# Taking the attention output out of PSUM with one ScalarE copy, and splitting it from SBUF

## The chip, the cores and the metric

The kernel runs on 1 core of one Trainium2 chip. The metric is the device time of one execution in microseconds (us); lower is better. The kernel before takes 699.35 us, the median of 3 runs (699.1 to 699.65).

## The reference

The computation is a sigmoid attention followed by a gated MLP with a spatial (token-mixing) gate, all in float32.

```python
# q, k, v: batch 8, 12 heads, 448 tokens, head dimension 64
scores = scale * np.matmul(q, k.transpose(0, 1, 3, 2)) - np.log(S)
attn = 1.0 / (1.0 + np.exp(-scores))
x = np.matmul(attn, v)            # then heads are joined: (8, 448, 768)

h = np.maximum(x @ w_in, 0.0)     # w_in: 768 x 1024
u, v = (h[..., :512], h[..., 512:])
v_n = (v - mean(v)) / np.sqrt(var(v) + 1e-06)
v_s = np.einsum('ts,bsd->btd', w_spatial, v_n) + b_spatial[None, :, None]
out = (u * v_s) @ w_out           # w_out: 512 x 768
```

## The kernel before

**Stages.** The eight batches are taken two at a time; the loop variable `m` counts the four pairs of batches. For each `m` the attention of both batches is computed into the SBUF tensor `x_s`, and then the MLP runs from `x_s`: `gate_values` (the half `v`, in PSUM tile `pv`), `spatial` (`pg`), `gated` (the half `u`, in `pu`) and `output` (`po`). The first attention pair of the next `m` is laid between the last outputs of this one.

**Precision.** Wide matmuls use operands in fp32r, and each operand is kept as a high part (the value rounded to fp32r) and a low part (the value minus the high part). `split(hi, lo, src, copy)` makes both: line 98 is the copy to the high part, on the engine that the caller names, and line 99 is a VectorE subtraction for the low part. The three products high*high, low*high and high*low are then added in PSUM.

**One attention step.** A unit is two heads of one batch; a batch has six units, and a step takes two units. So there are three steps for a batch, six for each `m`, and 24 in all. A step has seven score tiles, called here s (64 keys left over from both units, `t == NFULL`), e0, e1, e2 (the first unit) and o0, o1, o2 (the second). For each, `attention_scores` issues matmuls into a PSUM tile `psc` (line 251 for s, line 269, six matmuls a tile, for the others) and one ScalarE sigmoid (line 277) from there to an SBUF tile `at`. Then `attention_values` multiplies all seven `at` tiles with the values into one PSUM tile `pav` (line 295, 32 matmuls) in the order e0, e1, e2, o0, o1, o2, s; `pav` holds the first unit in one bank and the second in another. At its end `pav` is split into `x_s`, one unit after the other (lines 303 to 305): ScalarE makes the high part from PSUM, and VectorE the low part from PSUM and the high part.

**Buffers.** All PSUM tiles (`psc`, `pav`, `pv`, `pg`, `pu`, `po`) come from one pool of four buffers of two banks each, taken in turn. A step allocates eight of them, so `pav` stands in the buffer that e2 of the next step takes; o0, o1, o2 and the next `pav` take the buffers of that step's own s, e0, e1 and e2. The `at` tiles come from a pool `big` of `BIG = 7` SBUF buffers, taken in turn too; the tiles `vn` of `gate_values` come from the same pool.

**Order.** `in_program_order` keeps each engine's instructions in the order in which the program issues them. In one step that is: scores of s, e0, e1, e2, loads, scores of o0, o1, o2, in the first `m` a share of the weight preparation (`weigh`, on VectorE), the splits of q and k for the two units of the next step (`attention_splits`; the high part is made on ScalarE for batches 0 and 1 and on VectorE after that), and then `attention_values` with its split into `x_s`.

Of the kernel before, what the change touches and what calls it, by code (L numbers as in the profile page):

```python
# [8 lines left out]
F32 = mybir.dt.float32  # L9
# [5 lines left out]
P = 128  # L15
# [20 lines left out]
def attn_gmlp_kernel(  # L36
# [25 lines left out]
    nc = tc.nc  # L62
    B, NHP, _, _ = qk.shape
    S = out.shape[3]
# [15 lines left out]
    work = ctx.enter_context(tc.tile_pool(name="work", bufs=2))  # L80
# [7 lines left out]
    x_s = const.tile([P, 2, NCC, 2 * S], F32R, name="x_s")  # L88
# [8 lines left out]
    def split(hi, lo, src, copy):  # L97
        copy(hi, src)  # L98
        nc.vector.tensor_sub(lo, src, hi.bitcast(F32))  # L99

    def banks(name):
        return ps_2.tile([P, 2, 512], F32, tag="ps2", name=name)
# [3 lines left out]
    BIG = 7  # L106
# [173 lines left out]
    def attention_values(b, hp, ats):  # L280
        vt = values[b, hp]
        pav = banks(f"pav_{b}_{hp}")
        evens, odds = range(NFULL), range(NFULL + 1, TILES)
        for t in (*evens, *odds, NFULL):
            at = ats(t)
            for odd in range(2):
                if t == NFULL:
                    rows = slice(odd * HALF, (odd + 1) * HALF)
                elif (t > NFULL) == odd:
                    rows = slice(0, P)  # L290
                else:
                    continue
                for j in range(2):
                    heads = slice(j * D, (j + 1) * D)
                    nc.tensor.matmul(  # L295
                        pav[heads, odd, :S],
                        vt[rows, t, heads],
                        at[rows, j],
                        start=t == odd * (NFULL + 1),
                        stop=t == NFULL,  # L300
                    )
        cols = slice((b % 2) * S, (b % 2 + 1) * S)
        for odd in range(2):
            x, ps = x_s[:, :, hp + odd, cols], pav[:, odd, :S]
            split(x[:, 0], x[:, 1], ps, nc.scalar.copy)

    def product(ps, pairs, more=(), start=True, stop=True):

# [173 lines left out]
    def attention(m):  # L482
# [15 lines left out]
        for n in range(first, end, 2):  # L498
            if n:
                scores(n, short + evens)  # L500
            else:
                scores(n, evens)

            def loads():
                ahead(value_loads, n + 2, end)
                ahead(attention_loads, n + 4, end)
                ahead(attention_loads, n + 5, end)

            if n and n == first:
                yield  # L510
                attention_splits(*units[n + 1])
            if n:
                loads()
            scores(n, odds)
            if not n:
                scores(n, short)
            if n:
                weigh(WEIGH + (n + 2 == end))
            else:
                loads()  # L520
            ahead(attention_splits, n + 2, end)
            ahead(attention_splits, n + 3, end)
            if not n:
                weigh(1)
            attention_values(*units[n], lambda t: ats.pop((n, t)))
# [88 lines left out]
```

## Time and profile before

| | |
|---|---|
| median of 3 runs | 699.35 us |
| the profiled execution: its time / its span | 699.03 us / 697.2 us |
| TensorE matmul (PE) busy | 681.9 us, 98% of the span |
| TensorE weight load (PEld) busy | 505.9 us, 73% |
| VectorE (DVE) busy | 281.6 us, 40% |
| ScalarE (ACT) busy | 249.1 us, 36% |
| GpSimd (POOL) busy | 18.5 us, 3% |
| granted TensorE clock | 1.000 |

The span runs from the first to the last instruction, and the time of the execution has 1.83 us beside it. Matmuls are pipelined, so that the busy time of PE counts a matmul from its start to its modelled end, and several matmuls lie over one another. Idle time stands beside an instruction with the one that ended it. In the rows, "ACT x_s L98" is the copy to the high part of `x_s`, and "DVE x_s L99" the subtraction for its low part.

### The profile page before, as it was taken

The page shows a single profiled execution, that of the slowest core. Times are in us where ns is not written, and L with a number is a line of the kernel's source. Part 1 is how long each engine was busy: PE and PEld are TensorE (multiplying, and loading weights), DVE is VectorE, ACT ScalarE, POOL GpSimd, SP SyncE. Part 2 cuts the span into 40 slices and gives each one's busy share as a digit, 9 for nine tenths or more (in the row PEclk, how much of TensorE's full clock was granted, in tenths as well). Part 3 has the DMA queues.
Part 4 walks back from the last instruction along what each step waited for, and adds up shares of the span by engine and source line. Part 5 has one row for each costly group of instructions (what it writes and reads, how often), then busy time and mean ns, then how long its engine had stood idle before and what let it go on. Part 6 is the DMA issues. An engine that isn't in the chain of part 4 may idle for free.

```text
span 697.2 us, 9039 instructions
## 1 busy us (share of the span) xinstructions
PE 681.9 (98%) x3826; PEld 505.9 (73%) x3826; DVE 281.6 (40%) x445; ACT 249.1 (36%) x305; POOL 18.5 (3%) x36
## 2 busy tenths in 40 slices
PE   9999999999999999999999999999999999999997
PEld 3545789998645488999854458899985545889996
DVE  2767688833334037222242414621233431563020
ACT  5878322322466610011355741011136664101111
POOL 0000010000000001000000001100000000110000
PEclk9999999999999999999999999999999999999999
DMA  8754113160533000005062200000515410000102
GB/s 291 238 174 151 46 46 97 55 210 28 185 107 106 1 1 0 1 27 184 27 212 88 99 1 0 1 1 26 185 54 185 135 50 1 1 1 0 54 27 79
DMA packets 20552, 55.37 MB, mean 79 GB/s; under 512 B 1952, under 2 KB 8352, under 8 KB 20512
## 3 DMA queue, kind: packets, MB, share of 16 engines
q1 hardware_dynamic: 20224, 54.57, 23.0%
q8 instruction: 30, 0.49, 0.3%
q10 hardware_dynamic: 288, 0.23, 0.1%
q14 instruction: 10, 0.08, 0.0%
HBM read 43.78 MB, written 11.01 MB: 79 GB/s over the span
## 4 chain that ended last, share of the span: by engine, by line
PE 91%; DVE 4%; ACT 3%; issue 1%; DMA 0%
PE pav L295 20%; PE pu L311 17%; PE po L311 17%; PE pv L311 17%; PE psc L269 11%; PE pg L311 10%; DVE x_s L99 4%; ACT x_s L98 3%; PE psc L251 1%; DMA raw<-qk_dram 0%; DVE gs L99 0%; DVE g L428 0%; DVE osb L461 0%; ACT osb L459 0%; DVE gs L98 0%
## 5 line engine op out<-in xcount | busy, mean ns | idle before, releaser
L277 ACT ACTIVATE at<-psc,bias_s 128x896 f32<-128x896 f32 x168 | 153.9, 1026 | 22.1 <-PE psc L251 18.6
L295 PE MATMUL pav<-at,v 128*64 128x448 f32 (+1 forms) x768 | 135.4, 548 | 0.4
L311 PE MATMUL po<-gs,w_out_s 128*128 128x448 f32 x576 | 120.4, 368 | 1.0 <-DVE osb L461 0.9
L311 PE MATMUL pu<-x_s,w_in_s 128*128 128x448 f32 x576 | 118.0, 365 | 0.0
L311 PEld LDWEIGHTS po<-gs,w_out_s 128*128 128x128 f32 x576 | 107.7, 188 | 12.6 <-DVE osb L461 1.2
L311 PE MATMUL pv<-w_in_s,x_s 128*128 128x512 f32 x504 | 115.5, 390 | 0.0
L311 PEld LDWEIGHTS pu<-x_s,w_in_s 128*128 128x128 f32 x576 | 108.2, 188 | 8.6
L311 PEld LDWEIGHTS pv<-w_in_s,x_s 128*128 128x128 f32 x504 | 94.3, 188 | 22.3 <-issue 2.8
L269 PE MATMUL psc<-qks 64*128 64x448 f32 x828 | 99.1, 378 | 9.1 <-DVE x_s L99 9.1
L269 PEld LDWEIGHTS psc<-qks 64*128 64x128 f32 x828 | 75.4, 184 | 40.2 <-PE psc L269 16.1
L295 PEld LDWEIGHTS pav<-at,v 128*64 128x64 f32 (+1 forms) x768 | 44.2, 135 | 82.2 <-issue 62.0
L99 DVE TENSOR_TENSOR x_s<-pav,x_s 128x448 fp32r<-128x448 f32 x48 | 30.0, 625 | 142.4 <-ACT x_s L98 142.4
L311 PE MATMUL pg<-w_sp_s,vn 128*128 128x448 f32 x352 | 72.8, 365 | 0.0
L311 PEld LDWEIGHTS pg<-w_sp_s,vn 128*128 128x128 f32 x352 | 66.0, 187 | 5.8
L465 ACT COPY osb<-po 128x896 f32<-128x896 f32 x23 | 20.9, 907 | 114.4 <-PE po L311 97.8
L98 ACT CAST x_s<-pav 128x448 fp32r<-128x448 f32 x48 | 25.6, 532 | 86.2 <-PE pav L295 69.6
L99 DVE TENSOR_TENSOR qks<-raw,qks 128x832 fp32r<-128x832 f32 x46 | 46.7, 1025 | 19.3 <-ACT qks L98 18.1
L98 DVE CAST qks<-raw 128x832 fp32r<-128x832 f32 x36 | 21.2, 588 | 72.3 <-DMA raw<-qk_dram 37.1
L428 DVE SCALAR_TENSOR_TENSOR g<-pu,g 128x896 f32<-128x896 f32 x16 | 17.5, 1091 | 79.6 <-PE pu L311 79.6
L98 ACT CAST gs<-g 128x896 fp32r<-128x896 f32 x12 | 11.3, 943 | 99.0 <-DVE g L428 99.0
L346 ACT ACTIVATE rv<-pv 128x1024 f32<-128x1024 f32 (+1 forms) x16 | 14.6, 915 | 73.4 <-PE pv L311 73.4
L350 DVE BATCH_NORM_STATS2 stats<-rv 128x6 f32<-128x512 f32 x28 | 19.0, 679 | 38.4 <-ACT rv L346 38.4
(42 smaller groups left out, 243.3 us busy)
## 6 DMA issues: line engine op xcount, KB each, us to landing
raw<-qk_dram SPq DMA_DIRECT2D x48, 448.0 KB, 5.2
v<-v_dram SPq DMA_DIRECT2D x24, 448.0 KB, 3.3
out_dram<-osb SPq DMA_DIRECT2D x23, 448.0 KB, 2.6
wraw<-w_in_dram SPq DMA_DIRECT2D x12, 512.0 KB, 4.3
wraw<-w_out_dram SPq DMA_DIRECT2D x6, 512.0 KB, 3.6
wraw<-w_sp_dram SPq DMA_DIRECT2D x4, 256.0 KB, 4.8
b_bc<-b_sp_dram SPq DMA_DIRECT2D x1, 256.0 KB, 5.1
out_dram<-osb ACTq DMA_DIRECT2D x2, 112.0 KB, 1.7
```

The costliest lines, as they stand in the source:

```text
L98: copy(hi, src)
L99: nc.vector.tensor_sub(lo, src, hi.bitcast(F32))
L251: nc.tensor.matmul(psc[odd * HALF : (odd + 1) * HALF, j, :S], raw[rows, PART:], raw[rows, FULL:PART], start=True, stop=True,)
L269: nc.tensor.matmul(psc[:, j, :S], st[rows, k : k + P], mv[rows, FULL:PART], start=i == 0, stop=i == len(ops) - 1,)
L277: nc.scalar.activation(at, psc[:, :, :S], AF.Sigmoid, bias=bias_s, scale=QK)
L295: nc.tensor.matmul(pav[heads, odd, :S], vt[rows, t, heads], at[rows, j], start=t == odd * (NFULL + 1), stop=t == NFULL,)
L311: nc.tensor.matmul(ps, st, mv, start=start and i == 0, stop=stop and i == len(ops) - 1)
L346: nc.scalar.activation(rv[:, :n], pv[:, :n], AF.Relu)
L350: nc.vector.bn_stats(stats, rv[:, i])
L428: nc.vector.scalar_tensor_tensor(g, pu[:, :, :S], 0.0, g, op0=ALU.max, op1=ALU.mult)
L465: nc.scalar.copy(osb, po[:, :, :S])
```

## The change

In 20 of the 24 steps, one ScalarE copy takes both units' values (128 partitions by 896) from `pav` to a float32 tile `xf` in SBUF, which comes from the pool `big`; VectorE then makes the high part with a copy and the low part with a subtraction, both from `xf` and both over the two units at once. In the last step of each `m` (`hp + 2 == NHP` and an odd batch, 4 steps) there is no `xf`: the split reads PSUM as before, the high part on ScalarE and the low part on VectorE, but over both units in one instruction each.

```diff
         cols = slice((b % 2) * S, (b % 2 + 1) * S)
-        for odd in range(2):
-            x, ps = x_s[:, :, hp + odd, cols], pav[:, odd, :S]
-            split(x[:, 0], x[:, 1], ps, nc.scalar.copy)
+        x = x_s[:, :, hp : hp + 2, cols]
+        if hp + 2 == NHP and b % 2:
+            split(x[:, 0], x[:, 1], pav[:, :, :S], nc.scalar.copy)
+        else:
+            xf = work.tile([P, 2, 512], F32, tag="big", name=f"x_{b}_{hp}", bufs=BIG)[:, :, :S]
+            nc.scalar.copy(xf, pav[:, :, :S])
+            split(x[:, 0], x[:, 1], xf, nc.vector.tensor_copy)
```

## The prediction

> **What bounds the kernel now.** I read the page's busy shares and its chain of waits first, to see which engine sets the end.
>
> ```profile
> PE 681.9 (98%) x3826; PEld 505.9 (73%) x3826; DVE 281.6 (40%) x445; ACT 249.1 (36%) x305; POOL 18.5 (3%) x36
> ...
> PE 91%; DVE 4%; ACT 3%; issue 1%; DMA 0%
> PE pav L295 20%; PE pu L311 17%; PE po L311 17%; PE pv L311 17%; PE psc L269 11%; PE pg L311 10%; DVE x_s L99 4%; ACT x_s L98 3%; PE psc L251 1%; DMA raw<-qk_dram 0%; DVE gs L99 0%; DVE g L428 0%; DVE osb L461 0%; ACT osb L459 0%; DVE gs L98 0%
> ```
>
> The chain is nearly all PE. The one other thing on it is the split into x_s: 4% on DVE and 3% on ACT. Next, the table of waits of PE, and from the view of line 98 on ACT its own waits.
>
> ```profile
> PE psc L269 <- DVE x_s L99: 9.1, 20, 0.5
> ```
>
> ```profile
>   DVE x_s L99: 16.6, 24
> ```
>
> PE waits 20 times for the subtraction of x_s, 0.46 us each (9.1 / 20). That is every step but the last of each m: pav's buffer is needed by e2 of the next step. And ACT's second copy waits for VectorE's first subtraction (16.6 / 24 = 0.69 us): the split is a relay ACT, DVE, ACT, DVE. To see what else the relay holds up I take one step out of the timelines of ACT, PE (both around the second pair of batches) and PEld (around 17 to 21 us).
>
> ```profile
> 180.11 0.91 ACT L465 COPY osb<-po 128x896 f32<-128x896 f32 x1 [4.03 <-PE po L311]
> 180.93 2.80 ACT L277 ACTIVATE at<-psc,bias_s 128x896 f32<-128x896 f32 x3
> ...
> 198.89 0.53 ACT L98 CAST x_s<-pav 128x448 fp32r<-128x448 f32 x1 [3.07 <-PE pav L295]
> 200.12 0.53 ACT L98 CAST x_s<-pav 128x448 fp32r<-128x448 f32 x1 [0.69 <-DVE x_s L99]
> 200.54 6.40 ACT L277 ACTIVATE at<-psc,bias_s 128x896 f32<-128x896 f32 x7
> 210.02 0.53 ACT L98 CAST x_s<-pav 128x448 fp32r<-128x448 f32 x1 [3.07 <-PE pav L295]
> ```
>
> ```profile
> 201.45 2.85 PE L269 MATMUL psc<-qks 64*128 64x448 f32 x24 [0.46 <-DVE x_s L99]
> 204.31 5.64 PE L295 MATMUL pav<-at,v 128*64 128x448 f32 x32
> 209.77 0.93 PE L251 MATMUL psc<-raw 64*64 64x448 f32 x8
> 210.63 1.48 PE L269 MATMUL psc<-qks 64*128 64x448 f32 x12
> ```
>
> ```profile
> 16.59 1.11 PEld L269 LDWEIGHTS psc<-qks 64*128 64x128 f32 x12 [0.70 <-ACT x_s L98]
> 18.51 1.75 PEld L269 LDWEIGHTS psc<-qks 64*128 64x128 f32 x18 [0.81 <-PE psc L269]
> 20.50 0.50 PEld L269 LDWEIGHTS psc<-qks 64*128 64x128 f32 x6 [0.24 <-ACT at L277]
> 21.39 0.20 PEld L295 LDWEIGHTS pav<-at,v 128*64 128x64 f32 x4 [0.40 <-ACT at L277]
> ```
>
> A step takes 210.02 - 198.89 = 11.13 us. From here on I count from the start of the first ACT copy (198.89). PE's second stall hides behind the first: the weight load of pav waits 0.40 us for a sigmoid. pav takes e2's buffer, so it waits until the fourth sigmoid has read it. The seven sigmoids begin 0.895 us apart ((6.40 - 1.03) / 6, with 1.026 us for one in the groups below). The first begins at +1.65 (200.54), so the fourth ends at 1.65 + 3 x 0.895 + 1.03 = +5.36, and pav begins at +5.42 (204.31): the handover costs 0.06. So what sets a step is the loop pav, split, four sigmoids, pav. e2's stall is only the part of it that shows as an idle PE.
>
> **The change part by part.** The prices are those of the same engine, shape and memories, from the groups with shapes kept apart:
>
> ```profile
> L277 ACT ACTIVATE at<-psc,bias_s 128x896 f32<-128x896 f32 x168 | 153.9, 1026 | 22.1 <-PE psc L251 18.6 <-PE psc L269 3.5
> L99 DVE TENSOR_TENSOR x_s<-pav,x_s 128x448 fp32r<-128x448 f32 x48 | 30.0, 625 | 142.4 <-ACT x_s L98 142.4
> L465 ACT COPY osb<-po 128x896 f32<-128x896 f32 x23 | 20.9, 907 | 114.4 <-PE po L311 97.8 <-issue 10.3 <-DMA out_dram<-osb 6.3
> L99 DVE TENSOR_TENSOR gs<-g,gs 128x896 fp32r<-128x896 f32 x16 | 17.5, 1092 | 12.2 <-ACT gs L98 12.1
> L98 ACT CAST gs<-g 128x896 fp32r<-128x896 f32 x12 | 11.3, 943 | 99.0 <-DVE g L428 99.0
> L98 DVE CAST gs<-g 128x896 fp32r<-128x896 f32 x4 | 2.5, 626 | 0.1
> ```
>
> *ACT, 20 steps.* Two copies of 0.53 with a 0.69 wait go; one copy of 0.907 comes, and it waits for pav alone. What counts is when the first sigmoid can begin: +1.65 now. After a copy of just this form (PSUM, two banks, 128x896) a sigmoid begins 180.93 - 180.11 = 0.82 later. So the loop is shorter by 1.65 - 0.82 = **0.83 us a step**. s must be ready by then: its matmuls run from 209.77 for 0.93, to +0.68 of the step that begins at 210.02. It is.
>
> *pav's buffer* is free at +0.91 instead of after the second subtraction, and e2 comes when e0 and e1 (from +0.61) have been issued, which is after +1.7. So the 0.46 stall goes, with 0.8 to spare.
>
> *What PE itself needs.* When the stall goes, PE's own issue is the next bound. The chain has an undisturbed stretch of three such tiles:
>
> ```profile
> 163.08 2.02 PE psc L269 x18
> 165.10 14.98 PE po L311 x72
> ```
>
> Six tiles cost at most 2 x 2.02 = 4.04. The weight loads above give a lower price, (1.75 - 1.11) / 6 = 0.107 a matmul, so 2.02 + 18 x 0.107 = 3.95. From +0.61 (210.63, against the next step's zero of 210.02) pav could begin at +4.56 to +4.65. ACT allows it at 0.82 + 3 x 0.895 + 1.03 + 0.06 = +4.59. Both limits meet: against +5.42 the gain is 0.77 to 0.86, and I take ACT's 0.83. This is more than PE's idle of 0.46, because PE also issues more slowly while it waits for sigmoids tile by tile (24 matmuls take 2.85 instead of 24 x 0.107 = 2.57).
>
> The Trainium skill, "Trainium Kernel Development and Optimization", Performance Expectations, says that matmul busy time is a bad metric of how near a kernel is to its limit, since matmuls are pipelined. Going by PE's idle time alone, the sum would be 9.1 us; going by that rule, idle time is no cap on the gain, and the sum by the loop stands.
>
> *VectorE, 20 steps.* Two subtractions of 0.625 go; a copy of 0.626 and a subtraction of 1.092 come, 0.47 more work. From the second m on it has room, 6.15 us idle a step; the tight place is the first m, where weights are prepared too. Its timeline in both:
>
> ```profile
> 199.46 0.63 DVE L99 TENSOR_TENSOR x_s<-pav,x_s 128x448 fp32r<-128x448 f32 x1 [6.15 <-ACT x_s L98]
> ```
>
>
> ```profile
> 17.77 0.62 DVE L99 TENSOR_TENSOR x_s<-pav,x_s 128x448 fp32r<-128x448 f32 x1 [0.60 <-ACT x_s L98]
> 18.31 0.68 DVE L119 SCALAR_TENSOR_TENSOR wval<-wraw,wval 128x512 uint32<-128x512 uint32 x1
> ...
> 22.83 0.44 DVE L173 TENSOR_SCALAR wraw<-wraw 128x512 f32<-128x512 f32 x1
> 24.84 1.96 DVE L99 TENSOR_TENSOR qks<-raw,qks 128x832 fp32r<-128x832 f32 x2 [1.56 <-ACT qks L98]
> ```
>
> And ACT's there:
>
> ```profile
> 15.98 0.53 ACT L98 CAST x_s<-pav 128x448 fp32r<-128x448 f32 x1 [2.31 <-PE pav L295]
> 17.21 0.53 ACT L98 CAST x_s<-pav 128x448 fp32r<-128x448 f32 x1 [0.69 <-DVE x_s L99]
> 17.63 6.40 ACT L277 ACTIVATE at<-psc,bias_s 128x896 f32<-128x896 f32 x7
> 23.88 1.72 ACT L98 CAST qks<-raw 128x832 fp32r<-128x832 f32 x2
> ```
>
> From 15.98: the weight work queued behind the split begins at +2.33 (18.31) and lasts 4.96 (to 23.27). After the change the x copy begins at 0.91 + 0.04 = +0.95, the subtraction at about +1.6, and it ends at +2.7, so the weights run to +7.6. The q/k copies on ACT move with the sigmoids to 0.82 + 6.25 = +7.07, and VectorE's two subtractions of them follow 0.96 later, +8.03 to +9.99. A step will take 11.13 - 0.83 = 10.30, and the next x copy comes at +11.25. VectorE idles 0.4 us before the q/k work and 1.2 us before x, so nothing of the 0.47 reaches the path; without that cover it would cost up to 0.47 in 5 steps, 2.4 us. Bounds of the new copy: 0.626, or, if it ran like the subtraction, 1.09; then x is done at +3.2 and 0.7 of the room in front of x is left.
>
> *Waits that come.* xf takes the buffer of s's at tile, which the last matmuls of the same pav read; the copy waits for these anyway. o2's sigmoid of the next step now takes xf's buffer and waits for VectorE's subtraction, done at +2.7; its turn is at 0.82 + 6 x 0.895 = +6.2. Behind it stand only ACT's q/k copies and the next x copy. The other at tiles take buffers that pav freed earlier than now. Cost zero. No DMA moves by itself: the loads of q, k and v stand in SP's queue and wait for PE's reads, so they come 0.83 earlier a step along with their users.
>
> *The last step of each m (4).* One copy (0.907 to 0.943 by the nearest rows) and one subtraction of 1.092 end at about +2.1, against 17.77 + 0.62 - 15.98 = +2.4 now. PE goes straight on to pv with other columns of x_s and waits for neither, so 0.
>
> **Sum.** 20 x 0.83 = 16.6 us (15.4 to 17.2 by PE's two limits, 15.9 if the copy is as slow as 0.943). From the profiled execution: 699.03 - 16.6 = 682.4; the median of the runs lies 0.32 above that execution, so I say 682.6. Its own range is 681.2 to 684.0: at the one end the handover of 0.06 in front of pav goes too (20 x 0.89), at the other the gain is 15.4 from the median.
>
> **The rivals.**
>
> *Only the visible stall goes* (chance 0.10). PE gains the 9.1 us that the table of waits names and then waits for sigmoids as now: 699.35 - 9.1 = 690.2. For it: pav already waits for a sigmoid. Against: the same copy that frees pav also starts the sigmoids 0.83 earlier.
>
> *The first m gains nothing* (0.08). VectorE is fullest there; if its order of weights, q/k and x sets the step, 15 steps gain 0.83: 12.5 us, 686.9. For it: only 0.4 us idle left before the q/k work. Against: that work is needed by e0 only at about +10.9.
>
> *No change* (0.03). The split's relay leaves the path and another wait of the same size takes its place in every step, 699.3. Neither PE's nor ACT's rows show one; it is what remains if pav's buffer were still released by VectorE.
>
> *Slower* (0.05). One mechanism: the eighth tile in a ring of seven ties o2's sigmoid to VectorE. pav reads o2's at tile sixth of seven, at 4.59 + 5 x 5.64 / 7 = +8.6, so the subtraction from xf must end after 8.6 - 1.03 - 0.06 = +7.5 to delay PE, and after +8.3 to eat the gain. If VectorE did its weights and q/k work first (0.95 + 4.96 + 1.96 + 1.72 = +9.6) in each step, a step would be 1.3 longer than now: 20 x 1.3 = 26, 725. Against it: program order puts x in front of that work, and it ends at +2.7. The Trainium skill, "VectorE: DVE Perf Modes", Rules for kernel authors, advises to copy from PSUM to SBUF first only where many operations follow; here two follow, and by that rule the added VectorE time, 0.47 a step, is a loss, which the rows above hide.
>
> **How the numbers follow.** My forecast has 0.74. With the first-m rival it holds 0.82, so the range goes from 681.2 to 687.5 and leaves out the visible-stall rival, no change and slower. Differences under 0.2% (1.4 us) can't be told from none here. Faster: 0.74 + 0.10 + 0.08 = 0.92; same 0.03; slower 0.05.
>
> **What would show it.** The waits of PE should lose the x_s line, with nothing of its size in its place. A sigmoid should begin 0.82 after each x copy. The step should be 10.30 us instead of 11.13 in all four pairs of batches; 10.67 (11.13 - 0.46) would mean the first rival, and 11.13 in the first pair alone the second. ACT's copies should have 0.91, VectorE's 0.63 and 1.09. A wait of ACT at line 277 for VectorE's x_s would show the slower case. I am wrong if the step is held by something other than the sigmoid of e2 or PE's own issue.

## The result, and the profile after

The changed kernel takes 683.19 us (median; 682.8 to 684.21) against 699.35 for the kernel before. The ratio is 0.9771 with a 95% interval of 0.9754 to 0.9788: 2.3% faster. The profiled execution took 683.05 us, with a span of 681.3 against 697.2.

The page and PE's table of waits, after:

```profile
PE 675.0 (99%) x3826; PEld 504.9 (74%) x3826; DVE 290.5 (43%) x441; ACT 245.5 (36%) x281; POOL 18.5 (3%) x36
...
PE 98%; DVE 1%; DMA 0%; issue 0%; ACT 0%
```

```profile
PE warm L324 <- DVE zeros L320: 1.2, 1, 1.2
PE po L315 <- DVE osb L465: 0.9, 1, 0.9
```

The chain is now all PE: the split (7% before) has left it, and the x_s line has left the waits. Nothing of its size has come in its place. PE's busy time itself fell by 681.9 - 675.0 = 6.9 us with the same 3826 matmuls. That is the part of the gain that an idle count could not show.

One step of the changed kernel, in the timelines of ACT, PE and PEld around the second pair of batches:

```profile
193.84 0.91 ACT L308 COPY x<-pav 128x896 f32<-128x896 f32 x1 [3.12 <-PE pav L295]
194.65 6.40 ACT L277 ACTIVATE at<-psc,bias_s 128x896 f32<-128x896 f32 x7
204.17 0.91 ACT L308 COPY x<-pav 128x896 f32<-128x896 f32 x1 [3.13 <-PE pav L295]
```

```profile
188.08 5.64 PE L295 MATMUL pav<-at,v 128*64 128x448 f32 x32
193.54 0.93 PE L251 MATMUL psc<-raw 64*64 64x448 f32 x8
194.40 3.99 PE L269 MATMUL psc<-qks 64*128 64x448 f32 x36
198.41 5.64 PE L295 MATMUL pav<-at,v 128*64 128x448 f32 x32
```

```profile
198.41 0.20 PEld L295 LDWEIGHTS pav<-at,v 128*64 128x64 f32 x4 [0.39 <-ACT at L277]
```

A step is 204.17 - 193.84 = 10.33 us, from 11.13. The first sigmoid begins 0.81 after its copy. The 36 score matmuls run in one stretch of 3.99, which was 1.48, a stall of 0.46 and 2.85. The weight load of pav still waits 0.39 for a sigmoid. With the sigmoids 0.895 us apart, the fourth ends at 194.65 + 3 x 0.895 + 1.03 = 198.37, and pav begins at 198.41. So the loop of pav, copy and four sigmoids still sets the step, only shorter, although the chain names PE almost alone. ACT's copy begins 193.84 - (188.08 + 5.64) = 0.12 after pav's end. Before it was 210.02 - (204.31 + 5.64) = 0.07.

The new instructions, from the groups with shapes kept apart, and VectorE in the first m:

```profile
L308 ACT COPY x<-pav 128x896 f32<-128x896 f32 x20 | 18.1, 906 | 58.4 <-PE pav L295 58.4
L98 DVE CAST x_s<-x 128x896 fp32r<-128x896 f32 x20 | 12.6, 628 | 92.6 <-ACT x L308 92.6
L99 DVE TENSOR_TENSOR x_s<-x,x_s 128x896 fp32r<-128x896 f32 x20 | 21.8, 1092 | 0.7
```

```profile
16.64 0.63 DVE L98 CAST x_s<-x 128x896 fp32r<-128x896 f32 x1 [0.83 <-ACT x L308]
17.30 1.09 DVE L99 TENSOR_TENSOR x_s<-x,x_s 128x896 fp32r<-128x896 f32 x1
...
23.71 1.96 DVE L99 TENSOR_TENSOR qks<-raw,qks 128x832 fp32r<-128x832 f32 x2 [0.41 <-ACT qks L98]
26.97 0.63 DVE L98 CAST x_s<-x 128x896 fp32r<-128x896 f32 x1 [1.30 <-ACT x L308]
```

All three prices are those of the rows they were taken from (906, 628, 1092 ns), and VectorE keeps 0.41 us idle in front of the q/k work and 1.30 in front of x.

### The profile page after: what moved, and what is told of

Its sections match the earlier page's. It is cut to its first block, busy times and chain, and to the rows that moved or that the text cites. A ratio compares the mean times of both kernels' runs of the same rounds, so it can differ in the third digit from the quotient of the medians.

```text
span 681.3 us, 9034 instructions
## 1 busy us (share of the span) xinstructions
PE 675.0 (99%) x3826; PEld 504.9 (74%) x3826; DVE 290.5 (43%) x441; ACT 245.5 (36%) x281; POOL 18.5 (3%) x36
## 4 chain that ended last, share of the span: by engine, by line
PE 98%; DVE 1%; DMA 0%; issue 0%; ACT 0%
PE pav L295 20%; PE pu L315 17%; PE po L315 17%; PE pv L315 17%; PE psc L269 14%; PE pg L315 10%; PE psc L251 3%; DMA raw<-qk_dram 0%; DVE gs L99 0%; DVE g L432 0%; DVE osb L465 0%; ACT osb L463 0%; DVE gs L98 0%
## 5 line engine op out<-in xcount | busy, mean ns | idle before, releaser
L315 PEld LDWEIGHTS po<-gs,w_out_s 128*128 128x128 f32 x576 | 107.8, 188 | 12.5 <-DVE osb L465 1.2
L269 PE MATMUL psc<-qks 64*128 64x448 f32 x828 | 92.4, 372 | 0.0
L98 DVE CAST x_s<-x 128x896 fp32r<-128x896 f32 x20 | 12.6, 628 | 92.6 <-ACT x L308 92.6
L308 ACT COPY x<-pav 128x896 f32<-128x896 f32 x20 | 18.1, 906 | 58.4 <-PE pav L295 58.4
```

Source lines behind the costliest of these rows:

```text
L269: nc.tensor.matmul(psc[:, j, :S], st[rows, k : k + P], mv[rows, FULL:PART], start=i == 0, stop=i == len(ops) - 1,)
L308: nc.scalar.copy(xf, pav[:, :, :S])
L315: nc.tensor.matmul(ps, st, mv, start=start and i == 0, stop=stop and i == len(ops) - 1)
```

## The experiments

All runs of one group below ran on the same chip beside runs of the kernel before (medians 698.81, 698.91 and 699.22). The diffs are against the changed kernel.

**The changed kernel again.**

> The changed kernel as it is, for the runs beside it: 683.2, steps of 10.33 us.

> The changed kernel again, beside the run before: 683.1, 10.33 us a step.

It took 683.12 (ratio 0.9776, 0.9763 to 0.9790) and 683.44 (0.9777, 0.9763 to 0.9790).

**Does the start of the sigmoids set the step, or pav's buffer?** A second copy on ScalarE delays the sigmoids and leaves the buffer as it is; the shorter form copies only xf[:, 1] onto itself.

```diff
             nc.scalar.copy(xf, pav[:, :, :S])
+            nc.scalar.copy(xf, xf)
```

> The changed kernel with a second ScalarE copy of xf onto itself (128x896, SBUF to SBUF) behind the first in the 20 steps; the output is the same. pav's buffer is free as early as in the changed kernel; only the sigmoids come about 1.0 us later. My theory: a step takes about 11.3 us, 1.0 more, and the time is 701 to 704, slower than the kernel before, with no wait of PE for x_s in the table. Rival (only the wait for pav's buffer counts): 10.33 us a step and 683.2.

> The same with a second copy of one unit only (128x448 onto itself): the sigmoids come about 0.62 us later. My theory: a step of about 10.95 us and a time of 694.5 to 696.5, so that together with the longer copy the time goes one to one with the start of the sigmoids. Rival (only the wait for pav's buffer counts): 683.2.

The full copy took 702.15 us (ratio 1.0048, 1.0032 to 1.0064), the half 695.05 (0.9942, 0.9922 to 0.9962). ACT and PE with the full copy, and PE's waits:

```profile
199.62 0.91 ACT L308 COPY x<-pav 128x896 f32<-128x896 f32 x1 [3.12 <-PE pav L295]
...
201.40 6.39 ACT L277 ACTIVATE at<-psc,bias_s 128x896 f32<-128x896 f32 x7
```

```profile
193.85 5.64 PE L295 MATMUL pav<-at,v 128*64 128x448 f32 x32
...
205.15 2.10 PE L295 MATMUL pav<-at,v 128*64 128x448 f32 x10
```

```profile
PE psc L269 <- ACT at L277: 3.7, 20, 0.2
```

ACT and PE with the half copy:

```profile
198.18 0.91 ACT L308 COPY x<-pav 128x896 f32<-128x896 f32 x1 [3.12 <-PE pav L295]
...
199.59 6.39 ACT L277 ACTIVATE at<-psc,bias_s 128x896 f32<-128x896 f32 x7
```

```profile
192.41 5.64 PE L295 MATMUL pav<-at,v 128*64 128x448 f32 x32
...
203.34 2.85 PE L295 MATMUL pav<-at,v 128*64 128x448 f32 x14
```

From the copy to the first sigmoid it takes 0.81, 1.41 (199.59 - 198.18) and 1.78 (201.40 - 199.62); a step takes 10.33, 10.93 (203.34 - 192.41) and 11.30 (205.15 - 193.85). Added to the changed kernel that is 0.60 and 0.97 in front of the sigmoids, and 0.60 and 0.97 in the step: one to one. No wait for x_s stands in the table, and yet with the full copy the kernel is slower than the one before. This rules out that only the visible stall counted.

Both times lie in the ranges expected.

**Is the SBUF copy needed?** Two kernels without xf. The first uses the branch of the last step everywhere; the second keeps the four instructions of the kernel before and only puts both ScalarE copies first. The diffs show the lines that matter; the lines with xf are gone in both.

```diff
-        if hp + 2 == NHP and b % 2:
...
+        split(x[:, 0], x[:, 1], pav[:, :, :S], nc.scalar.copy)
```

> All 24 steps take the branch without xf: one ScalarE copy of both units to the high part and one VectorE subtraction for the low part, both from PSUM. My theory (the step is the loop pav, copy, four sigmoids, pav, with PE's own issue close behind): the sigmoids begin about 0.87 us after pav's end, as early as in the changed kernel, but pav's buffer is free only at 0.07 + 0.91 + 0.03 + 1.09 = 2.10 and e2 is due at 2.00, so PE is late by about 0.25; a step takes 10.46 to 10.53 us instead of 10.33 and the time is 686 to 687.5. Rival (only the wait for pav's buffer counts): the buffer is free 0.32 us earlier than in the kernel before, a step takes 11.13 - 0.32 = 10.81 and the time is 692.8.

```diff
-        x = x_s[:, :, hp : hp + 2, cols]
...
+        xs = [x_s[:, :, hp + odd, cols] for odd in range(2)]
+        for odd in range(2):
+            nc.scalar.copy(xs[odd][:, 0], pav[:, odd, :S])
+        for odd in range(2):
+            nc.vector.tensor_sub(xs[odd][:, 1], pav[:, odd, :S], xs[odd][:, 0].bitcast(F32))
```

> The four instructions of the kernel before (per unit, from PSUM, no xf) in another order: both ScalarE copies first, then both VectorE subtractions. My theory: the relay is broken, the sigmoids begin at 0.07 + 0.43 + 0.43 = 0.93 us after pav's end, the last subtraction ends at about 2.23, e2 is about 0.37 late and a step takes 10.55 to 10.62 us; time 687.5 to 689. Rival (only the wait for pav's buffer counts): 2.23 instead of 2.42, a step of 10.94, time 695.4. If the gain came from reading SBUF instead of PSUM on VectorE, nothing would be gained here: 699.

The merged split took 685.54 us (ratio 0.9810, 0.9793 to 0.9826), the other order 689.73 (0.9866, 0.9852 to 0.9881). ACT and PE of the merged split:

```profile
204.42 0.91 ACT L98 CAST x_s<-pav 128x896 fp32r<-128x896 f32 x1 [3.18 <-PE pav L295]
205.26 6.39 ACT L277 ACTIVATE at<-psc,bias_s 128x896 f32<-128x896 f32 x7
```

```profile
198.71 5.64 PE L295 MATMUL pav<-at,v 128*64 128x448 f32 x32
...
209.14 3.23 PE L295 MATMUL pav<-at,v 128*64 128x448 f32 x16
```

And PE of the other order, with its line in the table of waits:

```profile
200.79 5.64 PE L295 MATMUL pav<-at,v 128*64 128x448 f32 x32
...
208.81 2.71 PE L269 MATMUL psc<-qks 64*128 64x448 f32 x24 [0.20 <-DVE x_s L307]
211.44 2.85 PE L295 MATMUL pav<-at,v 128*64 128x448 f32 x14
```

```profile
PE psc L269 <- DVE x_s L307: 4.0, 20, 0.2
```

Their steps are 209.14 - 198.71 = 10.43 and 211.44 - 200.79 = 10.65. Of the change's 0.80 a step, the merged split has 0.70 and the mere order 0.48. So most of the gain is the end of the relay between the engines, which lets the sigmoids start early. The last 0.10 over the merged split comes with xf. It goes with pav's buffer, which ScalarE alone then frees before e2 is due, since the sigmoids follow pav's end as early in both (0.07 + 0.84 and 0.12 + 0.81). In the merged split PE's matmuls name no wait for the split, but the weight load of e2 does, 0.36 us in each of 20 steps, and the changed kernel has no such line:

```profile
PEld psc L269 <- DVE x_s L99: 7.2, 20, 0.4
```

Both expectations missed their ranges by a little. The merged split's step came out shorter than the 10.46 to 10.53 expected and its time 0.5 below 686; the other order's step came out longer than 10.55 to 10.62 and its time 0.7 above 689.

**What limits the step next?** VectorE takes the second unit out of PSUM, so that ScalarE's copy is half as long.

```diff
-            nc.scalar.copy(xf, pav[:, :, :S])
+            nc.scalar.copy(xf[:, 0], pav[:, 0, :S])
+            nc.vector.tensor_copy(xf[:, 1], pav[:, 1, :S])
```

> The 20 steps with both engines taking pav out: ScalarE copies the first unit to xf, VectorE the second, and the split from xf stays. ScalarE could begin its sigmoids 0.4 us earlier, but s is in PSUM only at 0.75 us after pav's end, so the first sigmoid begins at about 0.82 instead of 0.92. My theory: the gain is capped by this and by PE's own issue at 0.10 to 0.13 us a step; steps of 10.20 to 10.23, time 680.5 to 681.3. Rival (ScalarE's part of the loop is still the only limit): 0.37 us a step, 675.8. If VectorE's longer work costs more than this gives: 683 or above.

It took 683.20 us (ratio 0.9773, 0.9760 to 0.9787), the same as the changed kernel beside it (683.12). This expectation missed. ACT's timeline, and the first VectorE copy from its own:

```profile
194.52 0.53 ACT L308 COPY x<-pav 128x448 f32<-128x448 f32 x1 [3.12 <-PE pav L295]
195.30 6.40 ACT L277 ACTIVATE at<-psc,bias_s 128x896 f32<-128x896 f32 x7 [0.25 <-PE psc L251]
204.82 0.53 ACT L308 COPY x<-pav 128x448 f32<-128x448 f32 x1 [3.12 <-PE pav L295]
```

```profile
195.08 0.62 DVE L309 COPY x<-pav 128x448 f32<-128x448 f32 x1 [4.77 <-ACT x L308]
```

The shorter copy is followed by 0.25 us in which ACT waits for s (line 251). The first sigmoid comes 0.78 after the copy instead of 0.81. The cap was the right one, but I had put it 0.10 before the present start, and it lies only 0.03 before. The step is 204.82 - 194.52 = 10.30. The two engines did not take pav out at the same time: VectorE's copy waits for ScalarE's (195.08 against 194.52 + 0.53), although they read different banks, as ScalarE's second copy waited for VectorE's subtraction in the kernel before. Why the program puts one behind the other, no run shows.

**Can s be moved out of the loop?** s of the next step is scored in the middle of this step's pav, and pav takes s first (in the very first step, last as before). `between` calls `scores(n + 2, short)` if that step is in the same m, and the flags that start and end pav's sums go with the order.

```diff
-        for t in (*evens, *odds, NFULL):
+        order = (NFULL, *evens, *odds) if b or hp else (*evens, *odds, NFULL)
+        for t in order:
+            if t == NFULL + 2:
+                between()
...
-            if n:
-                scores(n, short + evens)
-            else:
-                scores(n, evens)
+            scores(n, short + evens if n and n == first else evens)
```

> The changed kernel, with s of the next step scored and sent through its sigmoid in the middle of this step's pav (behind o0) instead of behind it, and with pav taking s first instead of last; the first step of all keeps the old place. If, as the runs so far say, s and four sigmoids behind pav's end still set the step, this takes one sigmoid out of that loop, and PE's own issue becomes the only limit: 36 score matmuls and pav without a wait, 10.20 us a step, no more weight load of pav that waits for a sigmoid, and a time of about 680.5. Rival (PE's issue is the limit already, and the weight load's wait is only its mark): 10.33 and 683. If the changes between tile shapes on PE cost more than the wait did: above 683.5.

It took 685.89 us (ratio 0.9818, 0.9804 to 0.9831), slower than the changed kernel beside it (683.44). PE's timeline:

```profile
188.96 4.14 PE L298 MATMUL pav<-at,v 64*64 64x448 f32 x24
193.03 0.98 PE L251 MATMUL psc<-raw 64*64 64x448 f32 x8
193.94 1.73 PE L298 MATMUL pav<-at,v 128*64 128x448 f32 x8
195.60 3.91 PE L269 MATMUL psc<-qks 64*128 64x448 f32 x36
199.44 0.98 PE L298 MATMUL pav<-at,v 64*64 64x448 f32 x8
```

The 680.5 expected missed, and the last of the three outcomes named came. The scores did get shorter: from their first matmul to pav's it takes 199.44 - 195.60 = 3.84, against 198.41 - 194.40 = 4.01 in the changed kernel. The profile still puts the 0.30 us before pav's weight load down to a sigmoid, but PE loses nothing by it: pav begins 0.07 before the modelled end of the last score matmul (195.60 + 3.91 - 199.44), where in the changed kernel it begins 0.02 behind it (198.41 - (194.40 + 3.99)). But pav and s together take 195.60 - 188.96 = 6.64, against 194.40 - 188.08 = 6.32. The 64*64 tiles of pav and of s no longer lie side by side, and PE goes through two more changes of tile shape; I put the 0.32 us down to these, which no run tests alone. The step is 199.44 - 188.96 = 10.48. The Trainium skill, "TensorEngine Tiling (Array Packing)", Key Properties, states that a change of the tiling mode drains the TensorE; the rows agree, with 0.32 us for the two.

**How much room does VectorE have?** Four more subtractions a step, whose results are not used.

```diff
             split(x[:, 0], x[:, 1], xf, nc.vector.tensor_copy)
+            for _ in range(4):
+                nc.vector.tensor_sub(xf, xf, x[:, 0].bitcast(F32))
```

> The changed kernel with four more VectorE subtractions of 128x896 on xf behind the split in the 20 steps (their results are not used), about 4.2 us more VectorE work a step. My account of the cover: from the second m on VectorE idles 5.45 us a step, and xf is free at about 2.7 + 4.2 = 6.9 us, before the 7.5 from which o2's sigmoid would make PE late, so these steps stay at 10.33. In the first m VectorE idles only 1.7 us a step, becomes the bound, and its steps take about 12.8 us: the time is 683.2 + 4.5 to 5 x 2.5 = 694 to 696. Rival (the added VectorE work costs in every step): 683.2 + 20 x 2 or more = 723 or above. Rival (VectorE has room everywhere): 683.2.

It took 695.61 us (ratio 0.9953, 0.9934 to 0.9971), 12.5 more than the changed kernel. PE's table of waits, then ACT's, then PE's timelines in the first and in the second m:

```profile
PE psc L269 <- DVE qks L99: 5.9, 4, 1.6
PE pav L295 <- ACT at L277: 2.1, 4, 0.7
```

```profile
ACT at L277 <- DVE x L311: 23.8, 20, 1.8
```

```profile
58.81 3.98 PE L295 MATMUL pav<-at,v 128*64 128x448 f32 x20
63.43 1.89 PE L295 MATMUL pav<-at,v 128*64 128x448 f32 x12 [0.64 <-ACT at L277]
71.75 3.98 PE L295 MATMUL pav<-at,v 128*64 128x448 f32 x20
```

```profile
199.13 5.73 PE L295 MATMUL pav<-at,v 128*64 128x448 f32 x32
...
209.56 5.74 PE L295 MATMUL pav<-at,v 128*64 128x448 f32 x32
```

The time lies in the range expected. In the first m VectorE is the bound: the step shown takes 71.75 - 58.81 = 12.94. In the second the four subtractions, 4.47 us in VectorE's timeline, cost 209.56 - 199.13 - 10.33 = 0.10 a step, where none was expected. Two ways in which VectorE can hold a step are seen at work. In the first m the q/k parts come late (5.9 us), which is the way of the first-m rival. In all 20 steps o2's sigmoid waits for VectorE to leave xf (23.8 us), which is the way of the slower rival, and in the first m pav stops after its fifth tile for it.

## Why the prediction was right

682.6 us was predicted and 683.19 measured, inside the range and 0.6 above. By the prediction's own terms the sum is 699.35 - 16.6 = 682.75; and its own range takes the low end from the profiled execution and the high end from the median.

- **The loop.** The prediction named pav, split, four sigmoids and pav as what sets a step, with PE's stall only a part of it. The two delays of the sigmoids show this one to one. The visible-stall rival, 690.2, is out: steps of 10.67 would have been its mark, and they are 10.33.
- **0.83 a step.** It measured 0.80 (11.13 - 10.33). Two of its terms were off against each other. The sigmoid begins 0.81 after the copy, for 0.82. But the copy begins 0.12 after pav's end, where I had left the 0.07 of the old copy as it was.

The view of line 308 shows what stands there:

```profile
L308 ACTq EVENT_SEMAPHORE  x20: 17/17/17, 15.6 to 560.6; - x20
L308 ACT COPY x<-pav x20: 905/906/907, 15.7 to 560.7; 128x896 f32<-128x896 f32 x20
```

Each of the 20 copies has a semaphore instruction of its own in front. The program gives the copy two waits, for pav and for ScalarE's own earlier write to the same buffer of the ring, where a copy to x_s that comes first waits for pav alone. In the trace the wait for pav stands on the separate instruction: it runs 0.065 to 0.082 after pav's end, and the copy follows at 0.12. The copies that wait for pav alone start 0.07 after pav's end: all 24 of the merged split (204.42 - (198.71 + 5.64) in the rows above), and in the changed kernel itself the four of the last steps (67.28 - (61.57 + 5.64) for the first). A second wait does not always cost this. Copies of `osb` in the changed kernel have two waits as well, but there the separate instruction holds the older wait and is over long before the matmuls end. From the view of line 469 and the timelines of PE and ACT:

```profile
L469 ACTq EVENT_SEMAPHORE  x1: 17/17/17, 170.9 to 170.9; - x1
```

```profile
169.65 6.12 PE L315 MATMUL po<-gs,w_out_s 128*128 128x448 f32 x29
```

```profile
175.80 0.91 ACT L469 COPY osb<-po 128x896 f32<-128x896 f32 x1 [4.03 <-PE po L315]
```

This copy starts 175.80 - (169.65 + 6.12) = 0.03 after its matmuls. So the 0.05 goes with the wait for PE standing on an instruction of its own; like instructions are compared here, and no run moved that wait alone. The term of the sum that was mis-sized is thus the start of the copy. Under the waits that come, the prediction named only PE's reads of the buffer, "the copy waits for these anyway", at a cost of zero, and not how the waits are issued. 20 x 0.05 = 1.0 us.
- **PE's issue.** The prediction put PE's own limit at +4.56 to +4.65, beside ACT's +4.59, and called the two equal. The run with s moved has PE's scores without a wait at 3.84, so pav could begin at 0.61 + 3.84 = +4.45. Both of PE's prices, 3.95 and 4.04, were too dear; the forecast was spared, since it went by ACT's limit. Between the present step and PE's limit lie 4.01 - 3.84 = 0.17 us a step, 3.4 us in all; neither kernel that tried for it got there.
- **pav's buffer** left PE's waits as said. The two kernels without xf, whose e2 still waits for VectorE (0.36 and 0.20 a step), show that it needed both: an early copy, and a release that does not wait for VectorE.
- **VectorE's 0.47** cost nothing. The predicted idle times in the first m, 0.4 and 1.2, came out as 0.41 and 1.30. The rival that the first m gains nothing is out, since its steps are 10.33 too: the copies to x_s of two steps begin at 16.64 and 26.97. The Trainium skill, "VectorE: DVE Perf Modes", Rules for kernel authors, advises a copy from PSUM to SBUF first if many operations follow. Here two follow, VectorE got 0.47 us more a step (0.63 + 1.09 against 2 x 0.625), because it now makes the high part too, and the kernel is faster all the same: VectorE's own time did not decide.
- **The slower rival** named a real mechanism, but its limit of +7.5 was too late. With the four subtractions xf was free at 197.36 + 4.47 - 194.56 = +7.27, by VectorE's and ACT's timelines of the second m; o2's sigmoid waited 1.05 us for it, and the step cost 0.10. The weight loads of pav's sixth tile are due 191.51 - 188.08 = 3.43 after pav's start in the changed kernel, and not 5/7 of its 5.64 = 4.03.
- **The sum.** 20 x 0.80 = 16.0, and the span fell by 15.9. Two small things of this execution nearly cancel beside it: its first pav began at 9.94 instead of 10.27, and one step, whose first sigmoid was late, took 10.58. Each of the three profiles of this kernel has one such step of 10.58, and the other 19 are 10.33 to 10.34; why that one is longer stays open.

## What to carry to other kernels

Where one engine waits a little for another at a buffer, follow the chain once round the loop: the idle time of the busiest engine is only the first wait, and a second may stand behind it or beside it. A relay of two engines over the same PSUM tile makes each wait for the other; here putting both ScalarE copies first already brought 0.48 of the 0.80 us a step. One copy that empties the tile lets both the buffer and the engine behind it go, even if the other engine gets more work. Before giving the gain a price, find the next limit from an undisturbed stretch, for it decides how much a still shorter copy would bring.

## What was not expected of the hardware

A ScalarE copy whose wait for the matmuls stood on a semaphore instruction of its own started 0.05 us later than one that waited for them itself (0.12 instead of 0.07), though its other wait had long been met. The same shows behind s. With the half copy ACT was free, and the first sigmoid still began 195.30 - (194.22 + 0.93) = 0.15 after the end of s's matmuls, from the following row of PE's timeline. In the trace its wait for s stands on a separate instruction too. Three sigmoids of the changed kernel wait for s alone, and they begin 0.09 after it; the first of them 158.86 - (157.79 + 0.98).

```profile
194.22 0.93 PE L251 MATMUL psc<-raw 64*64 64x448 f32 x8
```
